# Infini-attention beside a 2-D FFT filter: the copies of the background products go right behind them, one part of the background list to a head step

## The chip, the cores and the metric

The kernel runs on one core of one Trainium2 chip. The metric is device microseconds of one execution. A core has five engines that work through their own instruction lists in order: TensorE (PE, matmuls; its weight loads are listed apart as PEld), VectorE (DVE), ScalarE (ACT), GpSimd (POOL) and SyncE (SP), which in this kernel only issues DMAs. They wait for each other by semaphores. Matmuls write to PSUM, of which this kernel uses eight banks of 128 x 512 floats in the stage of the change.

## The reference

Two independent computations, joined along the last axis. The second, `B`, is a real 2-D FFT of a 2048 x 576 array, a product with complex weights and the inverse FFT; the change leaves it alone. The first, `A`, is attention over S = 2048 tokens with 32 heads of 18 numbers in four segments of 512 tokens, plus a memory carried from segment to segment:

```
q, k, v = x@wq, x@wk, x@wv          # split in 32 heads, 4 segments
for s in range(4):
    p     = softmax(q_s k_s^T * 18**-0.5 + causal mask)
    a_dot = p @ v_s
    a_mem = (phi(q_s) @ M) / (phi(q_s) . z + 1e-6)      # phi(t) = t+1 if t>0 else exp(t)
    o_s   = g * a_mem + (1-g) * a_dot                   # g = sigmoid(beta), one per head
    M += phi(k_s)^T v_s ;  z += sum of phi(k_s)
out = o @ wo
```

## The kernel before, in words

The instructions of each engine run in the order in which the program writes them (the schedule is manual); generators are stepped by hand to interleave parts. The FFT, the projections of q, k and v and the inverse FFT fill the first 376 us. Then `attention` runs.

Attention works on "stacks" `n` (0 to 15): eight heads of one segment. A stack's `Qs` and `Ks` (three buffers each) are read from HBM by twelve DMAs on SP (`stack_dmas`, L588) and its values by a thirteenth (`load_v`, L594, three buffers); they are queued in the list `q` two stacks ahead. The loop `for t in range(133)` makes one **head step** per turn; a quad `k` is four heads, `hh` the head in the quad, so a stack takes eight steps, and a segment `g` 32. In a step:

- `s1(t+10)` in three parts: scores of a head ten steps ahead (L603), whose row maxima VectorE takes (L607) into `mg`. Its PSUM tag `s1` has three banks.
- `s2(t)` in three parts: scores of the present head (L641, L645, L646, L650) and their exponentials on ScalarE (L642, L647, L651) into `P`; with the last head of a quad four causal selects on POOL (L653). Tag `s2`, three banks.
- `pv`: four products of `P` with the values (L668), a quad behind; every fourth step `pv_out` copies the result to `U` (L674), which SP writes to HBM (`u_dmas`, L683 and L684, list `qu`).
- `mpath(k+2)`: at `hh==2` the maxima of a quad are transposed on TensorE (L622), copied twice by ScalarE (L626, L627) and written into row 108 of `Qs` by a DMA of POOL (L624); at `hh==3` VectorE takes the remainder (L630), which a second such DMA writes into row 109.
- up to two entries of `q` in the middle of the step and up to two of `qu`, else `q`, at its end.
- one turn of each generator in `lane` (`recip`: a reciprocal that goes through HBM, reads `rx`, `rr` and `rd`).
- `run_bg(1.6)`: on average 1.6 parts of the **background list** `bg`.

The background list holds `late_setup` (reads and splits `wo`) at the start, and from the 19th step of each segment on the work that closes the segment before:

- `combine(g-1)`, seven parts: spreads the reciprocal over the heads (`pb`, L762) and adds both kinds of attention on VectorE (L765, L767, L768), then splits the sum in a high and a low half (L757, L758). It reads `ux` from HBM (`ux_load`, L748, three buffers).
- five times `mem1`, two parts: the memory product (`pn`, L735), the read of the next segment's `pq` (L711), a copy on ScalarE (`am`, L739), the reciprocal's spread (`pb`, L741) and its product on VectorE (L742).
- `den(g+1)`, three parts: denominators (`pd`, L720), copied by ScalarE (`ds`, L722).
- `oproj(g-1)`, 25 parts: eight products with `wo`, each of 15 matmuls (`po`, L783) in three parts of five. A product's copy (`ob`, L787) and the store of each second one (`ya`, L788) are written behind the first five matmuls of the *next* product.

All of `pn`, `pb`, `pd` and `po` share the tag `post`, which has one bank, so a new tile's first matmul waits until the tile before it has been read. Behind the loop the rest of the list runs with the last reciprocal at 2.0 parts a turn, and then `combine(3)` and `oproj(3)` run by themselves.

Of the kernel before, what the change touches and what calls it, by code (L numbers as in the profile page):

```python
# [5 lines left out]
F32=mybir.dt.float32; F32R=mybir.dt.float32r  # L6
# [361 lines left out]
class ATT:  # L368
# [249 lines left out]
    def mpath(s,k):  # L618

        nc=s.nc; n,qd=divmod(k,2); Q=s.Qs[n%3]  # L620
        pt=s.psm.tile([128,512],F32,name="mt",tag=s.mtag)[:16,:128]
        nc.tensor.transpose(pt,s.mg.pop(k).rearrange("p h i -> p (h i)"),s.ident)  # L622
        mt=s.sm.tile([16,2,128],BF,name="mts")
        def put(a): nc.gpsimd.dma_start(Q[108+a:109+a,4*qd:4*qd+4].rearrange("p h (i c) -> p (h i) c",c=128),mt[:,a])  # L624
        mf=s.sm.tile([16,128],F32,name="mf")
        nc.scalar.copy(mf,pt)  # L626
        nc.scalar.copy(mt[:,0],mf)  # L627
        put(0)
        yield
        nc.vector.tensor_tensor(mt[:,1],mf,mt[:,0],op=OP.subtract)  # L630
        put(1)
        yield
# [80 lines left out]
    def den(s,g,lane):  # L713
        nc=s.nc; tp=s.tp
        ds=tp.tile([128,512],F32,name="ds",bufs=1); ds2=tp.tile([32,512],F32,name="ds2",bufs=1)
        for T,d in ((range(4),ds),((4,),ds2)):
            pd=s.ps.tile([128,512],F32,name="pd",tag="post")
            for t in T:
                r=126 if t<4 else 72
                nc.tensor.matmul(pd[32*(t%4):32*(t%4)+32],s.zst[g][:r,t],s.pq[g,t][:r],start=True,stop=True,skip_group_check=True)  # L720
            yield
            nc.scalar.copy(d,pd[:d.shape[0]])  # L722
        for t in range(5):
            w=7 if t<4 else 4
            nc.sync.dma_start(s.dD[g][7*t:7*t+w],ds[32*t:32*t+w] if t<4 else ds2[:w])
        def chain():
            yield
            yield
            yield from s.recip(s.dD[g],s.rdD[g],s.gt,True,"rd")
        lane.append(chain())  # L730
        yield
    def mem1(s,g,t):
        nc=s.nc; r=126 if t<4 else 72
        pn=s.ps.tile([126,512],F32,name="pn",tag="post")
        nc.tensor.matmul(pn[:r],s.Mst[g][:r,t,:r],s.pq.pop((g,t))[:r],start=True,stop=True)  # L735
        if g<3: s.pq_load(g+1,t)
        yield
        am=s.tp.tile([126,512],F32,name="am",bufs=5)
        nc.scalar.copy(am[:r],pn[:r])  # L739
        pb=s.ps.tile([126,512],F32,name="pb",tag="post")  # L740
        nc.tensor.matmul(pb[:r],s.sel[:,t,:r],s.rc["rd"],start=True,stop=True)  # L741
        nc.vector.tensor_tensor(am[:r],am[:r],pb[:r],op=OP.mult)  # L742
        s.am[t]=am
        yield
# [24 lines left out]
                if t<2: s.ux_load(g,t+3)  # L769
            yield  # L770
    def oproj(s,g):
        nc=s.nc; pend=None
        oh,ol=s.oh,s.ol
        for tb in range(4):
            ob=s.tp.tile([128,576],F32,name="ob")
            c=slice(128*tb,128*tb+128)
            for hf in range(2):
                ps=s.ps.tile([128,288],F32,name="po",tag="post")
                w=slice(288*hf,288*hf+288)
                L=[(a,b,t) for a,b in ((oh,s.woh),(oh,s.wol),(ol,s.woh)) for t in range(5)]  # L780
                for i,(a,b,t) in enumerate(L):
                    r=126 if t<4 else 72
                    nc.tensor.matmul(ps,a[t][:r,c],b[:r,t,w],start=i==0,stop=i==14)  # L783
                    if i==4 and pend: pend(); pend=None
                    if i%5==4: yield
                def pend(ob=ob,w=w,ps=ps,hf=hf,tb=tb):
                    nc.scalar.copy(ob[:,w],ps)  # L787
                    if hf==1: nc.sync.dma_start(s.io["ya"][g*512+128*tb:g*512+128*tb+128],ob)  # L788
        pend()
        yield  # L790
    def begin(s,sm,sp,ps1):
        s.sm,s.sp,s.ps1=sm,sp,ps1
        s.mg={};s.m2={};s.P={};s.vs={};s.rc={};s.am={};s.pq={};s.ux={};s.loaded=set()
    def prologue(s):

        for n in range(2):
            for i,f in enumerate(s.stack_dmas(n)):
                f()
                if i%4==3: yield
            s.load_v(n)  # L800
        for i in range(4): yield
        for t in range(10):
            yield from s.s1(t)
            if t in (4,8): m=s.mpath(t//4-1); next(m)
            if t in (5,9): next(m)
    def attention(s,tp,ps):
        s.tp,s.ps,s.psm,s.mtag=tp,ps,s.ps1,"s1"
        def steps(gen,i):
            for _ in range(i):
                try: next(gen)  # L810
                except StopIteration: return
        m=None
        q=[]
        qu=[]
        bg=[s.late_setup(tp)]
        state=dict(acc=0.0)
        def run_bg(rate):
            state["acc"]+=rate
            while state["acc"]>=1:
                state["acc"]-=1  # L820
                while bg:
                    try: next(bg[0]); break
                    except StopIteration: bg.pop(0)
        lane=[]
        for t in range(133):
            k,hh=divmod(t,4); n,qd=divmod(k,2); g=k//8
            if k<32 and hh==0 and qd==0 and n+2<16:
                q+=s.stack_dmas(n+2); q.append(lambda n=n: s.load_v(n+2))
            st=t%32
            if 16<=t<21: s.pq_load(1,t-16)  # L830
            if t==34: bg.append(s.den(1,lane))
            if st==10 and g>0:
                def ln(g=g):
                    yield from s.recip(s.rD[g-1],s.rrD[g-1],s.g1,False,"rr")
                    for u in range(3): s.ux_load(g-1,u)
                    for u in range(3): yield
                    bg.append(s.combine(g-1))
                    for u in range(5 if g<4 else 0): bg.append(s.mem1(g,u))
                    if g<3: bg.append(s.den(g+1,lane))
                    bg.append(s.oproj(g-1))  # L840
                lane.append(ln())
            a=s.s1(t+10) if t+10<128 else iter(())
            b=s.s2(t) if t<128 else iter(())
            steps(a,1)
            steps(b,1)
            steps(a,1)
            steps(b,1)
            if 4<=t-1<132: s.pv((t-5)//4,(t-5)%4)
            for _ in range(2):
                if q: q.pop(0)()  # L850
            steps(a,1)
            if hh==2 and k+2<32: m=s.mpath(k+2); next(m)
            steps(b,1)
            if hh==3 and m is not None: steps(m,1); m=None
            if t>=8 and t%4==0:
                s.pv_out((t-8)//4)
                if t%8==4: qu+=s.u_dmas((t-12)//8)
            for l in list(lane):
                try: next(l)
                except StopIteration: lane.remove(l)  # L860
            for _ in range(2):
                if qu: qu.pop(0)()
                elif q: q.pop(0)()
            run_bg(1.6)
        while q: q.pop(0)()
        while qu: qu.pop(0)()
        lane.append(s.recip(s.rD[3],s.rrD[3],s.g1,False,"rr"))
        while lane or bg:
            for l in list(lane):
                try: next(l)  # L870
                except StopIteration: lane.remove(l)
            run_bg(2.0)
        for u in range(3): s.ux_load(3,u)
        for _ in s.combine(3): pass
        for _ in s.oproj(3): pass
# [98 lines left out]
```

## Time and profile before

The runs took 879.1, 881.58 and 884.06 us (median 881.58).

| | |
|---|---|
| profiled execution | 884.07 us, span 882.1 us, mean granted TensorE clock 0.93 |
| busy over the span | PE 84%, DVE 66%, ACT 53%, POOL 21% |
| attention loop | 376 to 828 us |
| behind the loop | 828 to 882 us |

A page of the profile has parts: the busy time of each engine; the span in 40 slices; the DMA queues; the chain of work that ended last; the costliest groups of instructions; the DMA issues. Other views are made from the same trace: the waits (engine and line that waited, what released it, then microseconds in all, times, longest), the timeline (start, length, engine, line, operation, output<-input, count, and in brackets the idle time before it with its releaser), and tables of stretches of the span. L783 is line 783 of the kernel. The granted clock is the share of its full clock that TensorE was given.

### The profile page before, as it was taken

How to read it: one execution, taken by the hardware profiler on the slowest of the kernel's cores; microseconds unless marked ns; L12 is line 12 of the kernel's file. 1: busy time of each engine (PE TensorE's matmuls, PEld its weight loads, DVE VectorE, ACT ScalarE, POOL GpSimd, SP SyncE). 2: the span in 40 equal slices, each digit the busy share in tenths (PEclk: the TensorE clock that was granted, in tenths of full speed). 3: DMA queues.
4: the chain of work that ended last, by engine and by line, in shares of the span. 5: the costliest groups of instructions: out<-in, count | busy, mean ns of one | idle time of the engine just before them, and what ended most of it. 6: DMA issues, size and time to landing. Idle time of an engine off the chain costs nothing.

```text
span 882.1 us, 14645 instructions
## 1 busy us (share of the span) xinstructions
PE 742.6 (84%) x4751; PEld 495.3 (56%) x4751; DVE 584.8 (66%) x1687; ACT 466.5 (53%) x996; POOL 182.5 (21%) x339
## 2 busy tenths in 40 slices
PE   5988999999999699967777885888957798977856
PEld 4887797887979598922333331245512255422646
DVE  5998897977878799656665785546765565861040
ACT  3666966748565344346555664455644455664111
POOL 2110001010011644225332331122311121331000
PEclk9999999999999899978888998989977899989968
DMA  8873546445537685365654664534463345310121
GB/s 286 273 226 106 173 151 210 144 146 175 169 138 254 162 211 165 108 169 117 145 124 97 131 150 110 130 88 110 115 162 79 83 103 141 107 34 15 62 74 54
DMA packets 82463, 121.25 MB, mean 137 GB/s; under 512 B 9338, under 2 KB 49400, under 8 KB 82254
## 3 DMA queue, kind: packets, MB, share of 16 engines
q1 hardware_dynamic: 74836, 104.29, 42.3%
q0 software_dynamic: 7552, 16.03, 6.3%
q8 instruction: 38, 0.62, 0.3%
q14 instruction: 37, 0.30, 0.1%
HBM read 81.72 MB, written 38.35 MB: 136 GB/s over the span
## 4 chain that ended last, share of the span: by engine, by line
PE 57%; DMA 14%; DVE 11%; ACT 11%; issue 5%; POOL 1%; SPq 1%; ACTq 0%; DVEq 0%; POOLq 0%
PE pj L440 9%; PE po L783 8%; PE pv L668 8%; PE s L603 7%; PE pjv L440 7%; DMA Ks<-qkD 3%; DMA Qs<-qkD 3%; PE s L641 2%; DMA ux<-uD 2%; PE i L292 2%; PE i L303 2%; PE s L645 2%; PE pn L735 2%; DMA yb<-yout 2%; PE pm L497 1%
## 5 line engine op out<-in xcount | busy, mean ns | idle before, releaser
L607 DVE CUSTOM_DVE_ANT_0 junk<-s,mask 128x128 bf16<-128x128 f32 (+3 forms) x512 | 225.8, 485 | 118.0 <-PE s L603 116.2
L603 PE MATMUL s<-Ks,Qs 108*128 108x128 bf16 (+3 forms) x512 | 142.4, 323 | 27.4 <-DMA Ks<-qkD 10.5
L642 ACT ACTIVATE P<-s 128x512 f32<-128x512 f32 x128 | 76.4, 597 | 140.8 <-PE s L641 134.0
L603 PEld LDWEIGHTS <-Qs 108*128 108x128 bf16 x512 | 47.2, 102 | 130.0 <-issue 115.9
L668 PE MATMUL pv<-P,vs 128*32 128x512 f32 (+3 forms) x1024 | 104.8, 484 | 1.6 <-issue 1.1
L653 POOL TENSOR_SCALAR_AFFINE_SELECT P<-P 128x512 f32<-128x512 f32 x128 | 81.0, 663 | 50.9 <-ACT P L642 49.3
L624 POOL DMA_DIRECT2D Qs<-mts x64 | 31.7, 495 | 273.1 <-ACT P L651 229.3
L647 ACT ACTIVATE P<-s 128x512 f32<-128x512 f32 x128 | 76.0, 594 | 4.1 <-PE s L646 4.1
L440 PE MATMUL pj<-xh,wqkh 128*128 128x512 f32 x180 | 71.2, 395 | 0.5 <-ACT Z L151 0.5
L440 PE MATMUL pj<-xh,wqkl 128*128 128x512 f32 x180 | 71.1, 395 | 0.0
L651 ACT ACTIVATE P<-s 128x256 f32<-128x256 f32 x128 | 48.3, 377 | 31.1 <-PE s L650 30.1
L440 PE MATMUL pj<-xl,wqkh 128*128 128x512 f32 x144 | 61.8, 429 | 0.0
L641 PE MATMUL s<-Qs,Ks 110*128 110x512 bf16 x128 | 53.6, 418 | 6.5 <-DMA Qs<-mts 3.2
L202 DVE TENSOR_TENSOR Z<-t,t 128x290 f32<-128x290 f32 (+1 forms) x96 | 52.9, 596 | 0.2
L292 PE MATMUL i<-civ,Y 128*128 128x256 f32 (+1 forms) x288 | 44.5, 309 | 8.3 <-DVE T L320 4.6
L783 PE MATMUL po<-woh,oh 126*128 126x288 f32 (+1 forms) x160 | 32.7, 337 | 19.7 <-ACT ob L787 17.4
L202 DVE TENSOR_TENSOR t<-Z 128x580 f32<-128x580 f32 x64 | 48.0, 788 | 0.2
L440 PE MATMUL pjv<-wvh,xh 128*128 128x288 f32 x160 | 48.1, 303 | 0.0
L440 PE MATMUL pjv<-wvl,xh 128*128 128x288 f32 x160 | 46.2, 295 | 0.0
L292 PEld LDWEIGHTS i<-civ,Y 128*128 128x128 f32 (+1 forms) x288 | 39.8, 199 | 10.7 <-DVE T L320 5.9
L645 PE MATMUL s<-Qs,Ks 110*128 110x384 bf16 x128 | 45.3, 354 | 0.0
L607 DVE DVE_READ_ACCUMULATOR2_ANT mg<- 128x1 f32 x512 | 41.2, 80 | 0.0
(140 smaller groups left out, 1507.7 us busy)
## 6 DMA issues: line engine op xcount, KB each, us to landing
qkD<-sp SPq DMA_DIRECT2D x36, 384.0 KB
Qs<-qkD SPq DMA_DIRECT2D x96, 144.0 KB
Ks<-qkD SPq DMA_DIRECT2D x96, 144.0 KB
xin<-xb SPq DMA_DIRECT2D x16, 384.0 KB
cfw<-cfw POOLq DMA_DIRECT2D x16, 384.0 KB, 4.4
civ<-civ POOLq DMA_DIRECT2D x16, 384.0 KB, 6.9
vs<-vD SPq DMA_DIRECT2D x16, 330.0 KB
vD<-vt SPq DMA_DIRECT2D x16, 311.0 KB
```

What stands on the lines that cost most here:

```text
L202: v.tensor_tensor(o,a,b,op=op)
L292: nc.tensor.matmul(p[:m,k],Y[i][:,q,c*128:c*128+m],cc[:,hl,o:o+256],start=n==0,stop=n==5)
L440: s.nc.tensor.matmul(out,a,b,start=i==0,stop=i==len(L)-1)
L603: nc.tensor.matmul(out,Q[:108,h,128*i:128*i+128],K[:108,h,:128*(i+1)],start=True,stop=True)
L607: nc.vector.tensor_tensor_reduce(out=junk[:,:w],in0=src,in1=s.mask[:,512-w:],scale=1.0,scalar=-3.0e38, op0=OP.add,op1=OP.max,accum_out=s.m ...
L641: nc.tensor.matmul(p0,kk(0),q(0),start=True,stop=True)
L642: nc.scalar.activation(P[0][:,hh],p0,AF.Exp,scale=SC)
L645: nc.tensor.matmul(p1[:,:384],kk(1),q(128),start=True,stop=True)
L647: nc.scalar.activation(P[1][:,hh],p1,AF.Exp,scale=SC)
L653: sel=lambda x,pat: nc.gpsimd.affine_select(out=x,in_=x,pattern=pat+[[1,128]],compare_op=OP.is_ge,fill=0.0,base=0,channel_multiplier=-1)
L668: nc.tensor.matmul(s.pvt[32*hh:32*hh+32,128*j:],vt[:,j,19*h:19*h+32],mv[0][:,hh,mv[1]],start=jj==0,stop=jj==3,skip_group_check=True)
L783: nc.tensor.matmul(ps,a[t][:r,c],b[:r,t,w],start=i==0,stop=i==14)
```

## The change

Six edits, all in the attention part; no arithmetic changes.

- `mpath` yields once more, between the transpose and ScalarE's copies. In the loop the transpose stays ahead of the step's third part of `s2`, the copies and the first DMA go behind it, and the remainder with the second DMA goes ahead of the third part of `s1` at `hh==3`.
- `den` and `mem1`: the copy out of PSUM goes ahead of the yield; in `mem1` the read of `pq` goes behind the copy.
- `oproj`: a product is cut in two parts, eight and seven matmuls, 16 parts in all; its copy and store follow its last matmul.
- The loop takes up to two more entries of `q` at the start of a step.
- `run_bg` gets 1.1 in the loop and 1.0 behind it.

```diff
@@ mpath
         def put(a): nc.gpsimd.dma_start(Q[108+a:109+a,4*qd:4*qd+4].rearrange("p h (i c) -> p (h i) c",c=128),mt[:,a])
+        yield
         mf=s.sm.tile([16,128],F32,name="mf")
@@ den
                 nc.tensor.matmul(pd[32*(t%4):32*(t%4)+32],s.zst[g][:r,t],s.pq[g,t][:r],start=True,stop=True,skip_group_check=True)
+            nc.scalar.copy(d,pd[:d.shape[0]])
             yield
-            nc.scalar.copy(d,pd[:d.shape[0]])
@@ mem1
-        if g<3: s.pq_load(g+1,t)
-        yield
         am=s.tp.tile([126,512],F32,name="am",bufs=5)
         nc.scalar.copy(am[:r],pn[:r])
+        if g<3: s.pq_load(g+1,t)
+        yield
         pb=s.ps.tile([126,512],F32,name="pb",tag="post")
@@ oproj
-        nc=s.nc; pend=None
+        nc=s.nc
...
-                    if i==4 and pend: pend(); pend=None
-                    if i%5==4: yield
-                def pend(ob=ob,w=w,ps=ps,hf=hf,tb=tb):
-                    nc.scalar.copy(ob[:,w],ps)
-                    if hf==1: nc.sync.dma_start(s.io["ya"][g*512+128*tb:g*512+128*tb+128],ob)
-        pend()
-        yield
+                    if i==7: yield
+                nc.scalar.copy(ob[:,w],ps)
+                if hf==1: nc.sync.dma_start(s.io["ya"][g*512+128*tb:g*512+128*tb+128],ob)
+                yield
@@ prologue
-            if t in (4,8): m=s.mpath(t//4-1); next(m)
+            if t in (4,8): m=s.mpath(t//4-1); next(m); next(m)
@@ attention
+            for _ in range(2):
+                if q: q.pop(0)()
             steps(a,1)
             steps(b,1)
             steps(a,1)
@@
+            if hh==3 and m is not None: steps(m,1); m=None
             steps(a,1)
             if hh==2 and k+2<32: m=s.mpath(k+2); next(m)
             steps(b,1)
-            if hh==3 and m is not None: steps(m,1); m=None
+            if hh==2 and m is not None: steps(m,1)
@@
-            run_bg(1.6)
+            run_bg(1.1)
@@
-            run_bg(2.0)
+            run_bg(1.0)
```

More of the change, by code (lines that the diff above doesn't have):

```diff
@@ L735, in mem1 @@
         nc.tensor.matmul(pn[:r],s.Mst[g][:r,t,:r],s.pq.pop((g,t))[:r],start=True,stop=True)
+        am=s.tp.tile([126,512],F32,name="am",bufs=5)
+        nc.scalar.copy(am[:r],pn[:r])
         if g<3: s.pq_load(g+1,t)
         yield
-        am=s.tp.tile([126,512],F32,name="am",bufs=5)
-        nc.scalar.copy(am[:r],pn[:r])
         pb=s.ps.tile([126,512],F32,name="pb",tag="post")
```

## The prediction

> **What bounds the kernel now.** I read the page first, then the waits of TensorE in the attention loop (376 to 828 us), then a table of stages cut at the loop's own steps, then rows of the timeline, and last what SP's queue waits for.
>
> ```profile
> PE 742.6 (84%) x4751; PEld 495.3 (56%) x4751; DVE 584.8 (66%) x1687; ACT 466.5 (53%) x996; POOL 182.5 (21%) x339
> ```
>
> TensorE is the busiest engine over the span, but the first 376 us are projections and FFT, which the change does not touch. In the loop I cut at the first score product of each head step (L641). Columns are length, busy time of the engines, TensorE's granted clock, DMA share, GB/s:
>
> ```profile
> 376.48:523.32 146.84, 113.38 (x799) 45.60 (x800) 96.67 (x428) 86.03 (x195) 48.40 (x78) 0.86 0.58 133
> 523.32:543.35 20.03, 12.25 (x73) 4.43 (x70) 12.35 (x43) 8.17 (x19) 3.39 (x6) 0.83 0.55 122
> 543.35:577.03 33.68, 25.20 (x157) 8.92 (x155) 19.00 (x75) 18.18 (x41) 7.31 (x13) 1.00 0.44 109
> 577.03:634.80 57.77, 51.55 (x381) 29.66 (x380) 34.19 (x141) 29.93 (x69) 13.10 (x23) 0.94 0.44 107
> 634.80:642.74 7.94, 7.92 (x67) 3.36 (x65) 7.23 (x32) 6.38 (x15) 3.37 (x6) 1.00 0.68 171
> 642.74:666.36 23.62, 13.51 (x71) 4.44 (x70) 15.70 (x48) 8.54 (x21) 3.84 (x6) 0.71 0.53 125
> 666.36:707.27 40.91, 31.34 (x158) 10.23 (x155) 19.34 (x73) 18.23 (x41) 7.32 (x13) 0.83 0.33 88
> 707.27:761.05 53.78, 48.69 (x381) 28.78 (x380) 34.14 (x141) 29.38 (x68) 13.01 (x23) 1.00 0.49 116
> ```
>
> These are steps 0-50, then per group of heads: combine (4 steps), memory products with denominators (8), output products (16); four steps without background work at 634.80. Those four show the floor: 7.94/4 = 1.99 us a step, TensorE busy all of it and VectorE 1.81 us of it. Everything above 1.99 a step is the background list: 12.1, 17.8, 25.9 us for the first group, 15.7, 25.0, 22.0 for the second. TensorE's waits say how much of that is no work:
>
> ```profile
> PE pb L741 <- ACT am L739: 16.1, 15, 1.8
> PE po L783 <- ACT ob L787: 11.8, 17, 1.0
> PE pb L762 <- DVE ux L767: 11.3, 5, 6.0
> PE s L603 <- DMA Ks<-qkD: 10.5, 2, 5.3
> PE pb L762 <- DVE am L765: 7.7, 2, 6.8
> PE s L603 <- DMA pq<-pqD: 5.1, 1, 5.1
> PE s L603 <- DMA uD<-U: 4.5, 2, 3.8
> PE pn L735 <- DVE am L742: 3.9, 5, 0.8
> PE pd L720 <- ACT ds L722: 3.3, 3, 1.3
> ...
> PE s L603 <- DMA rD<-U: 2.3, 1, 2.3
> ```
>
> (Columns: total, times, longest.) Six of these are waits for the one PSUM bank that pn, pb, pd and po share: 54 us. The four of L603 for a DMA come in steps 5, 13, 21, 29 and 37, where the first scores of a newly read stack are due. How a wait for the bank arises:
>
> ```profile
> 715.06 0.39 ACT L787 COPY ob<-po 128x288 f32<-128x288 f32 x1
> 715.51 0.66 PE L783 MATMUL po<-woh,oh 126*128 126x288 f32 x3 [0.76 <-ACT ob L787]
> ```
>
> The product before ended near 712.5, but its copy was written behind the next product's first five matmuls, so it ran at 715.06, behind that step's exponentials, and TensorE stood.
>
> **The change, part by part.** The sum is made against the profiled execution, 884.1 us (span 882.1); the median shown, 881.6, is 2.5 lower.
>
> *Output products.* Counts of matmuls, copies and stores stay; a product is cut 8+7 over two steps instead of 5+5+5, and its copy and store go right behind it. ScalarE then does the 0.39 us copy while TensorE runs the next step's first score products, and the bank is free a step later. Fifteen matmuls cost 15 x 0.141 = 2.1 us (ten start at 812.02 and the next step at 813.43), eight products 16.9 us, against 25.9 and 22.0: gains 9.0 and 5.1. The copy now stands ahead of the next step's exponential on ScalarE. It ends some 0.46 us after the product; the score product that the exponential needs ends 0.6 us after it (two starts of 0.23, then 0.38 less overlap). Cost nothing; without that cover 0.4 us for each of 16, 6 us. The Trainium skill ("TensorE: Matmul & The Clock Gate", the table at its head) gives ScalarE a strict first-in-first-out queue, which speaks against such a copy; by the rule alone the sum would lose those 6 us and 9 more for the am copies.
>
> *Memory products and denominators.* The am and ds copies go ahead of the yield, so pb waits for nothing. With pn's pair at 0.73 us (a step of 2.63 against 1.90), pb 0.4, pd 1.9 for ten, VectorE's 0.69 us products partly beyond its 0.18 us slack: 5 x 1.13 + 1.9 + 1.4 = 9 us, against 17.8 and 25.0: gains 8.8 and 16. The second stage has the same instructions as the first and granted clock 0.83 against 1.00; I take full clock. The Trainium skill (same page, "HAM oscillation") has the clock halve after an idle gap of more than about 3.4 us; no wait in that stage is above 1.5 us, so trace and rule differ. By the rule the halving is not the waits' doing and the second gain is 9 instead of 16, the time 838, inside the forecast's own range. pq_load moves behind the am copy, on SP only, and is not late by that.
>
> *Rate 1.1, 1.0 at the end.* One part a step, two in every tenth. For combine it means pb waits a step, not VectorE's last product, and the ux reads (landing 9 us after issue at 528.74 and 650.32) have three steps to land instead of two. Left is VectorE's own work: five tiles x (0.68+0.69) - 7 x 0.18 = 5.6, later x (0.68+0.69+0.69) = 9.0, against 12.1 and 15.7: gains 6.5 and 6.7. Five of eight two-part steps still wait, at 0.9: minus 4.5. The list (36 parts a group instead of 45) now fills 33 of 32 steps, so the third group slips: steps 117-122 combine, 123-131 memory, and nearly all eight last products run behind the loop at 2.78 us each (836.95 less 834.15) instead of 4.3. Now 769.08 to 840.08 is 71.0 us. Then: two steps 3.5, combine 15.3 (2.5 a step without new scores), memory 18.4, last step 3, products 21-22: 62. Gain 8.5, bounded by 0 (the steps there do not shorten) and 16 (TensorE never waits). The reciprocal chain, 827.26 to 839.9, hides under the products.
>
> *Two more pops at the step's start.* SP's issue order alone: six stack reads a step for four. They pass wo, pq and rx reads. They start when the last scores free the slot, so the early rounds stay bound by the twelve reads (0.63 DMA share, 474 to 486). Gain where others stood between: 2.5 us (a wo read held SP 404.1 to 406.5), 1.7 (a pq read), and half-clock after: 5 together with den's 1. Bounds 0 and the 22 us of all DMA waits. The value read, too, moves from the middle of step 8n+3 to the start of 8n+2, and it holds SP until the pv of 8n+4:
>
> ```profile
> SPq L594 <- PE s L650: 53.0, 10, 9.2
> ```
>
> Behind it now: rx (steps 42, 74, 106; needed three steps later, two of them spent waiting) and one pq read, in step 98, issued at 100 and needed by den(3) at 100. I charge 4 us there, 0 for rx (VectorE has 1.5 steps), from nothing to 9.2 each.
>
> *Maxima.* mf and mts copies (0.25+0.30 us) go behind the 0.38 us exponential, transposes stay; the first DMA is 0.4 us later on POOL, the second goes ahead of 2.4 us of selects. They land 5.0 us after issue and are needed four steps later. The waits for it (3.2 us, steps 12, 20, 28) lie ahead of Ks waits: gain 0, bounds 0 and 3. POOL's selects wait for VectorE's subtraction, half a step early: nothing.
>
> *New waits.* Shorter steps meet the stack reads: 13.5 us and landing, some 15.5 us in six steps, 2.6 a step. Memory stages will run at 2.6 to 2.7, four rounds, 1.5 us each: minus 6.
>
> **Sum:** 9.0+5.1+8.8+12+6.5+6.7+8.5+5 = 61.6, less 4.5, less 6 (the 4 for den(3) is already in the 12): 51. 884.1-51 = 833; against the median 2.5 lower, 831 rounded. The unknown ends move it 15 either way.
>
> **Rivals.** *Other limits take the waits' place* (22%): VectorE at 1.81 of 1.99 us and the stack reads bound the steps once TensorE stops waiting. The early rounds show the price: waits of 5.2, 5.3, 5.1, 3.8, 2.3 us, mean 4.3, with 1.5 us of half clock behind. Six rounds at 5.8 give back 35 instead of 6: 860. For it: DMA share 0.44-0.55. Against: the loop's steps stay near 3.0 on average. *SP's queue makes it slower* (13%): the value read 1.5 steps earlier holds reads that TensorE or VectorE needs. At 3 us a step that is 4.5 us, in 14 rounds 63 us: 893. It decides from 3.7 us a round on. For it: 53 us in ten holds. Against: behind it stand few urgent reads. *More gain* (11%): no new waits, den(3) in time, clock full everywhere: 815. *The waits only covered work that comes due anyway* (4%): 880, no change by measurement.
>
> **How the numbers follow.** Forecast 831, chance 50%, its own range 816 to 846. The rival at 860 spans 846 to 876. The range 812 to 876 leaves out the slower case, the unchanged one and a little of the fastest. A measurement of this kernel tells about 0.5%, 4.4 us, from no change. Faster 50+22+11 = 83%, same 4%, slower 13%.
>
> **What would show it.** po's wait for ob gone in the loop, about half a microsecond each left behind it; pb's wait for am gone; combine without a 10 us step; granted clock near 1.00 in 523-707; seven to eight products in a row before the last combine. Wrong, if steps stay over 3.4 us on average, or TensorE's largest wait is for Ks or ux, or VectorE's ry waits for rx.

## The result and the profile after

The changed kernel takes 854.1 us (median of 848.6 to 856.31), the kernel before 882.48 us beside it (879.1 to 884.06): a ratio of 0.967, with a 95% interval of 0.962 to 0.973. A second set of runs, on another chip, gave 852.76 us and 0.969 (0.962 to 0.976). In two kernels of the experiments one execution of four, the profiled one, took 1686 and 2303 us, so these two have no trace that can be used; their medians count that execution, their ratios do not. The change saves some 28 us where the forecast had 51. 854 lies in the range of 812 to 876, but outside the likeliest case's own 816 to 846; it lies in the span of the rival in which other limits take the waits' place (846 to 876).

The profiled execution took 856.31 us, its span is 854.3 us, the mean granted clock 0.92. Below, the line of busy times of the page after: the work is the same, only the shares have grown, since the span is shorter.

```profile
PE 741.2 (87%) x4751; PEld 494.0 (58%) x4751; DVE 589.3 (69%) x1687; ACT 469.9 (55%) x996; POOL 181.2 (21%) x339
```

The stages of the changed kernel, cut at its own steps by the first score product (now L642): steps 0-50, then combine (7 steps), memory with denominators (11) and output products (15), for the first group of heads; 6, 12 and 15 steps for the second; from step 117 to the last combine; and the rest. Columns as in the table of before: length, busy times, TensorE's granted clock, DMA share, GB/s.

```profile
375.94:526.49 150.55, 116.90 (x799) 46.84 (x800) 97.18 (x428) 86.68 (x195) 48.13 (x78) 0.85 0.57 128
526.49:556.77 30.28, 23.19 (x120) 7.80 (x118) 20.88 (x69) 14.50 (x32) 6.75 (x12) 0.68 0.53 127
556.77:595.28 38.51, 31.54 (x206) 11.65 (x204) 23.87 (x99) 22.89 (x51) 10.12 (x18) 0.94 0.52 123
595.28:643.37 48.09, 46.98 (x365) 28.25 (x364) 32.42 (x133) 28.52 (x65) 11.05 (x20) 0.96 0.50 124
643.37:667.68 24.31, 21.29 (x105) 6.89 (x102) 18.76 (x59) 12.18 (x26) 6.28 (x11) 0.65 0.57 134
667.68:708.29 40.61, 34.90 (x222) 12.57 (x221) 26.27 (x109) 24.73 (x55) 10.11 (x18) 0.92 0.49 125
708.29:754.95 46.66, 45.05 (x365) 27.99 (x364) 32.71 (x135) 28.97 (x66) 13.49 (x24) 1.00 0.38 104
754.95:815.64 60.69, 50.30 (x318) 26.04 (x315) 19.63 (x33) 26.38 (x58) 8.16 (x14) 0.92 0.16 48
815.64:854.30 38.66, 23.34 (x125) 18.91 (x124) 9.71 (x15) 6.27 (x13) 0.00 (x0) 0.82 0.20 69
```

Two stages read as forecast: in the output products TensorE is busy 47 of 48 and 45 of 47 us. Two do not: in both combine stages the granted clock is 0.68 and 0.65, and in the two memory stages TensorE stands for 7 and 6 us of 39 and 41. TensorE's waits in the loop (376 to 785 us; total, times, longest) say on what:

```profile
PE s L603 <- DMA vs<-vD: 11.6, 2, 6.2
PE s L603 <- DMA uD<-U: 9.9, 2, 5.8
PE pd L721 <- DMA pq<-pqD: 9.9, 2, 6.1
PE s L603 <- DVE mg L607: 6.3, 8, 1.6
PE s L603 <- DMA rD<-U: 5.3, 1, 5.3
PE pb L763 <- DVE ux L768: 4.5, 1, 4.5
PE s L603 <- DMA Ks<-qkD: 3.0, 1, 3.0
...
PE po L784 <- ACT ob L786: 0.5, 1, 0.5
```

The waits of pb for the am copy (16.1 us before) and of po for the ob copy (11.8) have all but left the loop. In their place stand other waits. The lines of L603 for a DMA are the first scores of a newly read stack; the DMA named is the one that landed last ahead of it, mostly not the stack's own. They make 34.5 us, against 22.4 before. L603 also waits 6.3 us for VectorE's maxima (1.6 before). And one is new by its kind: pd, the denominators' product, waits 9.9 us in two places for `pq`. The first is in step 68, the second in step 100:

```profile
593.06 1.89 PE L721 MATMUL pd<-pq,zst 72*32 72x512 f32 x2 [6.12 <-DMA pq<-pqD]
```

SP's timeline of the same kernel shows why (start, length, what was issued, how many). The last of the five `pq` reads came behind all twelve reads of a stack:

```profile
574.59 0.32 SPq L712 DMA_DIRECT2D pq<-pqD  x1
574.96 2.28 SPq L588 DMA_DIRECT2D Qs<-qkD  x6
577.27 4.95 SPq L588 DMA_DIRECT2D Ks<-qkD  x6
583.18 0.30 SPq L712 DMA_DIRECT2D pq<-pqD  x1
586.68 0.39 SPq L594 DMA_DIRECT2D vs<-vD  x1
```

It was issued at 583.18, and the product that wanted it, idle from 586.9 on, could start at 593.06, 9.9 us later.

### The profile page after: what moved, and what is told of

It reads as the page before. It is cut to its first block, busy times and chain, and to the rows that moved or that the text cites. A ratio compares the mean times of both kernels' runs of the same rounds, so it can differ in the third digit from the quotient of the medians.

```text
span 854.3 us, 14652 instructions
## 1 busy us (share of the span) xinstructions
PE 741.2 (87%) x4751; PEld 494.0 (58%) x4751; DVE 589.3 (69%) x1687; ACT 469.9 (55%) x996; POOL 181.2 (21%) x339
## 4 chain that ended last, share of the span: by engine, by line
PE 56%; DMA 11%; DVE 11%; issue 10%; ACT 8%; POOL 2%; SPq 1%; DVEq 0%; ACTq 0%; POOLq 0%
PE pj L440 9%; PE po L784 7%; PE pv L669 7%; PE pjv L440 7%; PE s L603 7%; DMA Ks<-qkD 3%; PE i L292 2%; PE s L642 2%; PE i L303 2%; DMA Qs<-qkD 2%; PE s L646 2%; PE pn L736 2%; DMA pq<-pqD 2%; POOL P L654 1%; PE pm L497 1%
## 5 line engine op out<-in xcount | busy, mean ns | idle before, releaser
L603 PE MATMUL s<-Ks,Qs 108*128 108x128 bf16 (+3 forms) x512 | 146.2, 331 | 41.8 <-DMA vs<-vD 11.6
L603 PEld LDWEIGHTS <-Qs 108*128 108x128 bf16 x512 | 47.5, 103 | 151.1 <-issue 122.3
L669 PE MATMUL pv<-P,vs 128*32 128x512 f32 (+3 forms) x1024 | 107.4, 495 | 2.2 <-issue 1.1
L654 POOL TENSOR_SCALAR_AFFINE_SELECT P<-P 128x512 f32<-128x512 f32 x128 | 76.9, 640 | 17.4 <-ACT P L643 17.1
L642 PE MATMUL s<-Qs,Ks 110*128 110x512 bf16 x128 | 55.3, 432 | 3.3 <-ACT P L643 2.5
L669 PEld LDWEIGHTS pv<-P,vs 128*32 128x32 f32 x1024 | 21.4, 113 | 35.1 <-issue 26.9
```

The source lines that it names most:

```text
L603: nc.tensor.matmul(out,Q[:108,h,128*i:128*i+128],K[:108,h,:128*(i+1)],start=True,stop=True)
L642: nc.tensor.matmul(p0,kk(0),q(0),start=True,stop=True)
L654: sel=lambda x,pat: nc.gpsimd.affine_select(out=x,in_=x,pattern=pat+[[1,128]],compare_op=OP.is_ge,fill=0.0,base=0,channel_multiplier=-1)
L669: nc.tensor.matmul(s.pvt[32*hh:32*hh+32,128*j:],vt[:,j,19*h:19*h+32],mv[0][:,hh,mv[1]],start=jj==0,stop=jj==3,skip_group_check=True)
```

## The experiments

Two theories stood at the start. The one of *order*: the two pops at the start of a step put a whole stack's reads on SP ahead of small reads that TensorE needs sooner, the last `pq` read above all, and that costs what is missing. The one of a *floor*: once TensorE stops waiting for the copies, the reads of the stacks set the pace, whatever their order. Ratios are to the kernel before on the same chip, as chips differ by half a per cent.

**Without the pops.** The changed kernel, less

```diff
-            for _ in range(2):
-                if q: q.pop(0)()
```

> The changed kernel without the two more pops at the step's start; nothing else differs. Theory ORDER (SP's new issue order, with the value read 1.5 steps earlier, is what ate the gain): the first 51 steps go back from 150.6 to 147 us, the 3.8 us wait of the denominators in step 100 goes, 845 to 849 us. Theory FLOOR (the twelve stack reads run at their own pace of 0.63 of the DMA engines from the moment the slot is free, whatever the order): 852 to 856, waits of L603 for DMAs still 25 us or more.

Measured: 839.35 us, ratio 0.949 (0.944 to 0.954), against 0.967 for the whole change: by the medians the pops cost some 15 us. The 839 is below the ranges of both theories. What FLOOR said of the waits holds all the same: L603 waits 34.6 us for DMAs here, as much as the 34.5 in the whole change, so these waits are not what the pops made longer. SP's order in the same place, and the product that waited, in the profile without pops:

```profile
563.70 0.32 SPq L712 DMA_DIRECT2D pq<-pqD  x1
564.06 2.27 SPq L588 DMA_DIRECT2D Qs<-qkD  x6
566.37 0.99 SPq L588 DMA_DIRECT2D Ks<-qkD  x2
569.06 0.30 SPq L712 DMA_DIRECT2D pq<-pqD  x1
569.41 3.28 SPq L588 DMA_DIRECT2D Ks<-qkD  x4
...
576.88 1.02 PE L721 MATMUL pd<-pq,zst 72*32 72x512 f32 x2 [0.83 <-DMA pq<-pqD]
```

The `pq` read now slips in between the second and the third `Ks` read, and the wait is 0.83 us instead of 6.12: it is issued 7.0 us ahead of the moment when pd wants it and lands 7.8 us after its issue, where the changed kernel has 3.8 and 9.9. The stage (steps 58 to 68) takes 32.3 us where the two profiles of the whole change have 38.5 and 38.3. So 6 of the 15 us are seen in this place. At step 100, where ORDER had the wait go, 2.69 us are left of 3.75. From step 58 to the end the two profiles of the whole change agree (297.5 and 297.7 us), and the one without pops takes 291.0; ahead of step 58 the same two differ by 7 us (180.8 and 173.6 from the first step on). So 6.6 us are the pops' in the traces, and the rest of the 15 lies in a stretch that varies by about as much from one execution to the next.

**The value reads late.** The changed kernel with the pops, but the value read out of `q`:

```diff
-                q+=s.stack_dmas(n+2); q.append(lambda n=n: s.load_v(n+2))
+                q+=s.stack_dmas(n+2)
+            if n+2<16 and t%8==6: s.load_v(n+2)
```

> The changed kernel with the value read of a stack issued in step 8n+6, behind the pv that it has to wait for, so it never holds SP's queue (before: 50.6 us of holding in ten waits). ORDER: the pq read of step 98 goes out 4 to 6 us earlier, U's stores and the later ux reads too; den(3)'s wait of 3.8 us and the half-clock step behind it go, 847 to 850. FLOOR: nothing that TensorE waits for stood behind the value read but that one; 851 to 855.

Measured: 845.64 us, 0.954 (0.949 to 0.959). Some gain, though pd still waits 8.1 us for `pq`; what is shorter in its trace is steps 0-50 (140.5 us against 150.6 and 148.6), and that stage turns out to vary by itself (below). From step 58 to the end it takes 299.3 us, no less than the whole change.

**The copies alone.** The kernel before with the three edits that put copies (and `pq_load`) right behind the products and cut the output products in two; old rates, no pops, old path of the maxima:

```diff
@@ den
+            nc.scalar.copy(d,pd[:d.shape[0]])
             yield
-            nc.scalar.copy(d,pd[:d.shape[0]])
@@ mem1
-        if g<3: s.pq_load(g+1,t)
-        yield
...
+        if g<3: s.pq_load(g+1,t)
+        yield
@@ oproj
-                    if i==4 and pend: pend(); pend=None
-                    if i%5==4: yield
...
+                    if i==7: yield
+                nc.scalar.copy(ob[:,w],ps)
```

> The kernel before with the copies alone: am, ds and ob copies right behind their matmuls, a product in two parts; rates 1.6 and 2.0, no more pops, maxima as before. Theory COPIES (the gain is the waits of TensorE for am, ds and ob, 16.1+11.8+3.3 us in the loop): 858 to 864. Theory RATE (spreading the list is what gains, the copies alone meet the bank again in steps with two parts): 870 to 880.

Measured: 853.37 us, 0.961 (0.956 to 0.965), 34 us less than before on that chip. That is more than was expected here, and as much as the whole change gives. The other three edits together add nothing that can be told from zero.

**The old rates.** The changed kernel with

```diff
-            run_bg(1.1)
+            run_bg(1.6)
...
-            run_bg(1.0)
+            run_bg(2.0)
```

> The changed kernel with the old rates 1.6 and 2.0. RATE: combine's waits for VectorE's products (19 us) and ux come back, 866 to 874. COPIES: the rate changes little, 852 to 858; the denominators come earlier in the list's round, before the stack reads of the next round, so their waits for pq (9.9 us) should go, which may even make it 847 to 850.

Measured: 859.23 us, 0.970 (0.962 to 0.977), not to be told from the whole change at 0.967: with the pops in place the lower rate brings nothing. The waits of pd for `pq` are gone in its trace, as expected, and yet it is no faster. It differs from the copies alone (0.961) by the pops and the path of the maxima, and it is 5.9 us slower, with intervals that just overlap. So a price of the pops where pd does not wait for `pq` is not excluded.

**The change once more**, as a base for the second chip:

> The changed kernel once more, on one chip with the next three, so that the price of its parts is taken on one chip: 0.965 to 0.970 of the kernel before. If the chip were what made the kernel without the pops look better, it would be near 0.95 here.

Measured: 852.76 us, 0.969 (0.962 to 0.976). The `pq` waits at steps 68 and 100 are there again, 5.78 and 4.05 us.

**Both: no pops, and the value reads late.**

```diff
-            for _ in range(2):
-                if q: q.pop(0)()
...
+            if n+2<16 and t%8==6: s.load_v(n+2)
```

> The changed kernel without the two pops and with the value read behind the pv that frees its slot. Theory ORDER: the pops cost in two ways, by what stands behind twelve stack reads (pq, ux) and by the value read's earlier hold; without the pops a hold of SP is left for 5 us a round, so this gains a little more, 0.940 to 0.947 of before (2 to 7 us under the kernel without the pops). Theory POPS ONLY: the hold by itself costs nothing that TensorE waits for, 0.947 to 0.951.

Measured: 839.75 us, 0.951 (0.945 to 0.957), the same as without pops alone. Without the pops the place of the value read is worth nothing that can be measured.

**The pops alone**, in the kernel before:

```diff
+            for _ in range(2):
+                if q: q.pop(0)()
             steps(a,1)
```

> The kernel before with the two pops alone. If the pops cost wherever they stand: 1.010 to 1.020 of before. If they cost only where the denominators come at the time of the stack reads (rate 1.1): 0.998 to 1.005, since the old rate has the denominators in steps 61 and 93, before the reads of steps 64 and 96. My forecast's own price for them was a gain of 5 us, 0.994.

Measured: 884.55 us, 1.001 (0.997 to 1.005). The same edit that costs 15 us in the changed kernel costs nothing in the old one. In its trace the denominators run in steps 61 and 62, ahead of the stack reads that start with step 64, and pd waits for no `pq`; in the changed kernel they run in steps 67 and 68, behind them.

**No pops and the old path of the maxima.** The changed kernel less pops, and less the extra yield of `mpath` with its places in the loop:

```diff
-        yield
...
-            if hh==3 and m is not None: steps(m,1); m=None
...
-            if hh==2 and m is not None: steps(m,1)
+            if hh==3 and m is not None: steps(m,1); m=None
```

> The changed kernel without the pops and with the maxima's copies and DMAs where they were. It splits the 14 us between the copies alone and the kernel without the pops into rate and maxima. My forecast priced the maxima at 0 to 3 us: 0.948 to 0.952 of before. If the maxima are what gains (the exponential no longer behind two copies that wait for a transpose): 0.957 to 0.962.

Measured: 836.71 us, 0.951 (0.945 to 0.958), as without pops alone (0.949): the maxima are worth nothing measurable. The traces show an exchange: on the old path TensorE waits 5.9 us for the row of maxima (`mts`) and 3.8 us at L603 for VectorE's maxima, on the new one (without pops) not at all and 7.4. Against the copies alone (0.961) this kernel has only the lower rate more: some 8 us, with intervals that overlap a little.

**The denominators later, with the pops kept.** If the lateness of `pq` is the whole price, it must go when its reader moves away. `den(g+1)` goes behind the first three output products:

```diff
+                    o=s.oproj(g-1)
+                    def first(o=o):
+                        for _ in range(6): next(o); yield
+                    bg.append(first())
                     if g<3: bg.append(s.den(g+1,lane))
-                    bg.append(s.oproj(g-1))
+                    bg.append(o)
```

> The changed kernel, pops kept, with the denominators moved behind the first three products of the background list (six parts later), when the pq reads have long landed. If the pops cost by the pq read that they put behind the twelve stack reads (waits of 6.1 and 3.8 us and the half clock behind them): 840 to 844, 0.953 to 0.958 of before, and the waits of pd for pq are gone. If they cost mainly elsewhere (early rounds, combine): 849 to 853.

Measured: 837.07 us, 0.945 (0.940 to 0.951): below both ranges: with all pops in it, as fast as any kernel here that does the whole computation.

**The denominators later, without the pops**, both edits together:

> The changed kernel without the pops and with the denominators behind the first three products: what is left there is 3.5 us of waits for pq and a step at half clock. 0.941 to 0.946 of before, 4 to 6 us under the kernel without the pops. If the wait only moves to the stack's first scores: 0.947 to 0.951.

Measured: 837.26 us, 0.946 (0.940 to 0.952). With the unmoved denominators the ratios are: pops 0.967 and 0.969, no pops 0.949; with the moved ones: pops 0.945, no pops 0.946. So at the new rate the pops cost some 15 us where the denominators stand near the stack reads, and nothing that can be measured where they do not. That ties the cost to the place of the denominators, but it does not account for each microsecond: the trace of the last kernel has no wait of pd for `pq` left, and there is no usable one for the kernel with the pops kept. From step 58 to the end the last kernel takes 280.7 us, against 291.0 without the move. So the move is worth some 10 us there even without pops; in the profiled times it is hidden, because this execution took 181.8 us ahead of step 58 and the other 170.7, with the same instructions.

**Reads of sixteen rows.** Why do the stack reads take so long? The Trainium skill ("DMA: Bandwidth & Descriptors", "How many engines (k)" under the section on semaphores) has a DMA from SP run on the largest number of engines up to 16 that divides its slowest dimension: 9 for the 18 rows of a stack read. The kernel without pops, with each read cut in 16 rows and 2:

```diff
-                ap=bass.AP(tensor=a.tensor,offset=a.offset,ap=[[1536,18],[1536*18,8],[1,512]])
-                L.append(lambda T=T,pc=pc,ap=ap: nc.sync.dma_start(T[18*pc:18*pc+18],ap))
+                ap=bass.AP(tensor=a.tensor,offset=a.offset,ap=[[1536,16],[1536*18,8],[1,512]])
+                ap2=bass.AP(tensor=a.tensor,offset=a.offset+16*1536,ap=[[1536,2],[1536*18,8],[1,512]])
...
+                    nc.sync.dma_start(T[18*pc:18*pc+16],ap)
+                    nc.sync.dma_start(T[18*pc+16:18*pc+18],ap2)
```

> The changed kernel without the pops, each stack read of 18 rows cut in one of 16 rows and one of two (24 DMAs a stack). Theory FLOOR: the stack reads run at 0.63 of the DMA engines because a read of 18 rows is spread over nine of them, and the remaining waits of TensorE for stacks (some 30 us with the half clock behind them, before step 60) follow from that; with 16 the share in the reads goes to 0.85 or more, those waits fall to a half or less: 0.920 to 0.935 of before. If the reads are bound elsewhere, or SP's 24 issues at 0.38 us take their place: 0.947 to 0.960.

Measured: 892.19 us, 1.010 (1.005 to 1.014), 6% slower than without the cut and outside both ranges. The reads of one stack in this kernel, from the first issue on, and in the kernel without pops (the last two columns are the DMA share and GB/s):

```profile
472.00:489.00 17.00, 11.90 (x99) 4.92 (x96) 11.15 (x54) 10.48 (x24) 6.50 (x12) 0.94 0.54 109
```

```profile
473.00:488.00 15.00, 13.96 (x108) 4.96 (x105) 11.07 (x52) 11.52 (x25) 6.25 (x11) 1.00 0.64 141
```

Fewer GB/s were moved, and the twenty-four reads were issued over 14 us, where the twelve took 6.6. In another round the share was higher with the cut than without (0.75 at 446 to 456 us against 0.67 at 451 to 463), and still fewer GB/s were moved (132 against 142). If the rule holds here, more engines for most of each read did not help, at twice the number of DMAs; no run shows on how many engines a read ran. Whether sixteen rows would help at the same number of DMAs is open.

**Half the reads.** The kernel without pops, in which stacks from the fourth on read only their even pieces:

```diff
+                if n>=3 and pc%2: continue
```

> The changed kernel without the pops, and from the fourth stack on only six of a stack's twelve reads are made (the other rows keep an older stack's numbers: that part of the computation is left out). FLOOR: from step 13 on the waits for stacks are gone, and with them the half clock behind them: 0.915 to 0.930 of before. If the waits were SP's order or latency rather than the amount read: 0.940 to 0.950.

Measured: 811.71 us, 0.919 (0.914 to 0.924), against 0.949, in FLOOR's range: 26 us hang on the amount read. Steps 0-50 in this kernel, and in the one without pops:

```profile
376.34:499.38 123.04, 105.78 (x800) 44.35 (x801) 96.51 (x428) 85.56 (x195) 48.30 (x78) 0.93 0.51 124
```

```profile
375.07:521.46 146.39, 112.25 (x799) 45.48 (x800) 97.16 (x428) 85.86 (x195) 48.16 (x78) 0.87 0.57 133
```

The two profiles differ by 23.4 us in steps 0-50, which have little background work and which take as long in the kernel before (146.84). From there to the end they differ by 6.6 us (315.2 against 308.6). So the floor exists, but nearly all of it was there before the change; only the small part is a wait that the change can have uncovered. A fourth buffer for the stacks, which would let the reads start sooner, was not tried.

## Why the prediction was right or wrong

Gains by stage in us of span, forecast and measured; the forecast charged waits at the two-part steps (4.5) and at the stack reads (6) in a lump, while the measured ones lie in the rows. A stage's gain is its length over 1.99 us a step, before less after; the last row but one runs to the end of the span. The sum of the column for the change is the difference of the spans, 27.8, but for rounding.

| stage | forecast | the change | without pops |
|---|---|---|---|
| steps 0-50, with the start | 5 | -3.2 | 1.9 |
| combine | 13.2 | -1.0 | 4.4 |
| memory and denominators | 20.8 | 9.4 | 16.7 |
| output products | 14.1 | 12.8 | 13.2 |
| end | 8.5 | 9.8 | 9.3 |
| new waits | -10.5 | in the rows | in the rows |
| sum | 51 | 27.8 | 45.5 |

*Output products: right.* 16.9 us of extra time was forecast for each eight; 48.09 and 46.66 less fifteen plain steps of 1.99 leave 18.2 and 16.8. Of the 1.3 more in the first, 0.7 come with a step of 4.90 us at a granted clock of 0.64, right behind the wait for `pq`; without the pops this step takes 4.23. The copies cost nothing, as the rows show: the end of a product, its copy, the next step's first score product and exponential, and the next product, from the timeline after.

```profile
737.00 0.83 PE L784 MATMUL po<-woh,ol 126*128 126x288 f32 x5
...
737.87 0.40 ACT L786 COPY ob<-po 128x288 f32<-128x288 f32 x1
737.90 0.38 PE L642 MATMUL s<-Qs,Ks 110*128 110x512 bf16 x1
738.32 0.60 ACT L643 ACTIVATE P<-s 128x512 f32<-128x512 f32 x1
...
739.16 0.91 PE L784 MATMUL po<-woh,oh 126*128 126x288 f32 x5
```

The exponential starts 0.42 us behind its score product's start, as it does at 735.27, where no copy stands just ahead of it, and the next product has no idle time in brackets. The 6 and 9 us by which a first-in-first-out ScalarE would have cost did not appear. Behind the loop the copies of two products start at 803.72 and 806.50, 2.78 us apart, as worked out.

*Memory: right; denominators: wrong at one, right at the other.* pb's wait for the am copy is down to 1.1 us. The 4 us charged at den(3) are there: its `pq` read was issued at 698.61, right behind a value read at 698.18, and the product waited 3.75 us. But den(2) in step 68, charged nothing, waited 6.12.

*The step that failed* is the term "Two more pops at the step's start", with its bounds of "0 and the 22 us of all DMA waits", and beside it the sentence that `pq_load` "is not late by that". It was taken as a gain of 5 and cost, by the medians, some 15: a miss of 20 of the 23 us between 831 and 854. The bound below left out a loss, although the text itself counted what else stands on SP. The forecast did ask what is held behind the value read, and forgot to ask what is held behind the twelve reads that now go out in one run. And it costed the pops and the rate apart; the pops alone cost nothing (1.001), and in the changed kernel, where one part a step brings the denominators to the time of a stack's reads, they cost 15 us. That the rate is the whole reason is not shown, since the changed kernel at the old rates was no faster (0.970). Of these 15 us, 6.6 are seen behind step 58, nearly all at step 68. The rest is not placed: it would have to lie in steps 0-50 and in the first combine, where the profiles of the whole change (150.6 and 148.6; 30.3 and 25.0) differ from the one without pops (146.4; 24.3) by hardly more than two kernels without pops and with the same instructions there differ from each other (146.4 and 24.3; 152.1 and 29.7 in the one whose denominators are moved, which takes effect only later).

*Without the pops the sum held,* closer than its rows. The other terms add to 46, or 50 without the charge for the value read; measured 48.4 (839.35 against 887.71 on that chip), or 45.4 between the two profiles. In the rows combine and memory together gained 12.9 us less than forecast, and the two lumps of 10.5 us charged for waits cover most of it; that the lumps had this size is partly luck. (The 0.63 of the DMA engines that the forecast gives for 474 to 486 us is that of 475 to 486; the other is 0.62.) The copies' terms add to 35; measured 34. The maxima were put at nothing; 0.951 against 0.949.

*Rate: the size half right, the place wrong.* Combine was to gain 13.2 less 4.5 and gained 4.4 without the pops. Its waits for VectorE's last product (10 us steps) did go in the first two groups (one of 4.5 us is left in the third, at step 119), but steps 53 and 85 now wait for a stack (5.47 and 3.02 us), and half clock follows. The lump of 6 us for new waits at the stack reads is about what the half reads give behind step 50, 6.6.

*Rivals.* The rival whose span holds 854 was the right kind, other limits in the waits' place, but not the right one, so that 854 falls in its span, and in the whole range by way of it, is luck. Its mechanism was stack reads at 5.8 us in six rounds, and with the pops gone the same kernel takes 839 with all of those reads in it. What cost the time between the forecast and the result was mostly the order on one queue. One of the forecast's signs of being wrong did come, that TensorE's largest wait is for a stack: it is L603's, 34.5 us; but it is as large without the pops, at 839. The rival on the other side put 63 us on the value read that holds SP; put late it gives back some 12 by the ratios with the pops (0.954 against 0.967 and 0.969), which its trace does not show behind step 58, and nothing without them.

*The clock.* The forecast took full clock from 523 to 707; it was 0.68 and 0.65 in the combine stages. The Trainium skill ("TensorE: Matmul & The Clock Gate", "HAM oscillation") halves the clock behind gaps of more than about 3.4 us. That agrees with step 53 (5.47) and less well with step 85 (3.02, and the clock at 0.50 from 652 to 660 us), and not with what is shown in the last section.

The best kernels here are the change without its pops and the change with the denominators three products later, at ratios of 0.945 to 0.951, some 2% below the change itself; which of them is best can't be told.

## What to carry to other kernels

When an edit changes when a queue issues, list every small read that comes behind the run of large ones and the step that needs it, after all the other edits have moved that step; an edit that is free by itself can cost some 15 us beside others. Where a stretch repeats from one execution to the next to a few tenths of a microsecond, price an edit by that stretch and not by the median of the whole. Waits taken away by copies put behind their products were worth about what the waits' own lines said (34 us measured, 31 in the lines); gains that rest on transfers coming earlier were worth nothing here. And halving a transfer in an experiment, wrong numbers and all, tells in one run how much hangs on it, and in which stage.

## What the runs showed of the hardware that was not expected

The clock was halved behind short waits too. In the changed kernel TensorE waited 1.44 us until 506.1 and 1.89 us until 512.6; the stretches there read (granted clock third from the end):

```profile
510.00:512.00 2.00, 0.68 (x6) 0.11 (x2) 0.60 (x4) 0.56 (x2) 0.06 (x1) 1.00 1.13 200
512.00:514.00 2.00, 1.43 (x10) 0.68 (x14) 0.37 (x1) 0.79 (x2) 0.00 (x0) 0.87 0.25 72
514.00:516.00 2.00, 1.39 (x9) 0.10 (x1) 1.90 (x7) 0.29 (x1) 0.00 (x0) 0.50 0.37 94
516.00:518.00 2.00, 1.75 (x6) 0.77 (x7) 1.67 (x9) 0.92 (x4) 0.00 (x0) 0.50 0.45 114
```

The step there (from 512.8) took 4.43 us; with the value reads late, where the clock stayed at 1.00, the same step took 3.39. Without the pops a wait of 1.17 us, alone, left the clock at 1.00. The length of a wait does not settle it: the same wait of 1.44 us in step 43 left the clock at 1.00 in the changed kernel (505 to 512 us) and was followed by 0.50 (504 to 506 us) without the pops. And the half clock can last: in the first combine of the change it stood at 0.50 from 539 to 553 us behind a wait of 5.47, with another of 1.62 near the end of that stretch, where the second profile of the same kernel shows 0.86 for the stage.

```profile
539.00:547.00 8.00, 8.00 (x35) 2.58 (x35) 4.48 (x17) 4.03 (x10) 0.49 (x1) 0.50 0.19 57
547.00:553.00 6.00, 4.38 (x20) 1.51 (x20) 5.93 (x14) 3.15 (x7) 2.88 (x5) 0.50 0.55 120
```

A stack read cut in two came out worse than whole, even with the larger part in sixteen rows (109 against 141 GB/s in the reads of one stack). What sets the pace of the stack reads stays open.
